# Two small reads ahead of and behind the load of c at the start of a DiT block

## The chip, the cores and the metric

The kernel runs on one core of one Trainium2 chip. The metric is the device time of one execution in microseconds; where several executions are given, it is their median. The profile is of one further execution, recorded by the hardware profiler; times in it count from the first instruction (the start of the span).

The engines are named as the profile names them: PE (TensorE: matmuls and transposes; PEld is its weight load), DVE (VectorE), ACT (ScalarE), POOL (GpSimd) and SP (SyncE, which only issues DMAs here). ACT and SP each issue DMAs on a queue of their own, q10 and q1 in the profile.

## The reference

The reference is one block of a diffusion transformer with adaptive layer norm, for 2 batches of 256 tokens, width D = 1152, 2 heads of 576, and an MLP of width 4608:

```python
mod = (_silu(c) @ w_mod).reshape(B, 6, 1, D)
shift_a, scale_a, gate_a, shift_m, scale_m, gate_m = [mod[:, i] for i in range(6)]
h = _layernorm(x, axis=-1) * (1 + scale_a) + shift_a
qkv = (h @ wqkv).reshape(B, N, 3, H, Dh)
q, k, v = (qkv[:, :, 0].copy(), qkv[:, :, 1].copy(), qkv[:, :, 2].copy())
attn = _softmax(jnp.einsum('bqhd,bkhd->bhqk', q, k) * Dh ** (-0.5), axis=-1)
a = jnp.einsum('bhqk,bkhd->bqhd', attn, v).reshape(B, N, D) @ wo
x = x + gate_a * a
h2 = _layernorm(x, axis=-1) * (1 + scale_m) + shift_m
m = _gelu(h2 @ w_fc1) @ w_fc2
return x + gate_m * m
```

All inputs are bfloat16. c has only 2 rows of 1152 values, but everything after the first layer norm depends on it through mod.

## The kernel before, in words

Tokens are held in four tiles of 128 partitions: tile t holds batch t // 2, and partition p of batch b holds the tokens 2p and 2p + 1, so one partition's two tokens are 4608 contiguous bytes in memory and one tile's row is 2304 bytes. Weights are held as nine chunks of 128 rows (KD = 9).

All weights and x are loaded by SP, in the order in which the program lists them: the four tiles of x in the order 0, 1, 3, 2 (L86), then alternating pieces of w_scale_a (the columns of w_mod for scale_a, L107) and of w_k (the K columns of wqkv, rows of chunk 0, chunk 1, then pairs of chunks, L104), then w_shift_a, w_q, w_gate_a, w_v, w_o and the rest. SP does nothing else, so that this order is the order of its queue. ACT issues the load of c (c_sb, 18 rows of 256 bytes, L84) as its first instruction, then loads its table of functions (L153).

The order of work on every engine is the order in which the program calls it: a loop at the end of the kernel ties each instruction to the one before it on its engine. At the start, that order is:

- PE: two warming matmuls of zeros in float32 (L173; each is two records in the profile, so 4), the transpose of c into pc (L176), seven more warming matmuls (14 records), the transposes of the first chunks of the normalized x of batch 0 (L264), the products of w_scale_a with silu(c) for chunks 0 and 1 (L245, L247), then the K projection in steps over the chunks (L280), with further transposes and scale groups between the steps.
- ACT: the load of c, the table load, the exponential of pc for silu (L178), then the sum and the sum of squares of x tile 0 (L206, two passes with a read of the accumulator after each), the square roots by logarithm and exponential (L335, L351, L338), then the same for tile 2.
- DVE: the rest of silu (L179 to L181, which writes sT), the statistics of x tile 1 (L193, L195), a small product for tile 0 (L213), the statistics of tile 3, then the normalizations xn of tiles 1 and 0 (L233), later of 3 and 2, and the modulations.
- POOL: constants, and small steps of the means and roots.

So tiles 0 and 2 get their statistics on ACT and tiles 1 and 3 on DVE. The lines of the load and of the transpose of c:

```python
nc.scalar.dma_start(c_sb[:], c_v)                                   # L84
...
warm(2, pwarm)
nc.tensor.transpose(pc[:], c_sb[:], ident[0:B * KD, 0:B * KD])      # L176
nc.scalar.activation(sig[:], pc[:], ACT.Exp, scale=-1.0)            # L178
...
warm(7, pwarm)
act_stats(0)
```

Completion of DMAs from ACT and SP is counted on eight semaphores, which the framework hands out in turn over all of these DMAs in program order; a DMA that gets a semaphore again waits, on the engine that issues it, for the DMA that had it before, unless a wait already made covers that.

The pieces that the diff touches and what is around them:

Of the kernel before, what the change touches and what calls it, by code (L numbers as in the profile page):

```python
# [9 lines left out]
BF16 = mybir.dt.bfloat16  # L10
# [9 lines left out]
def kernel(  # L20
# [11 lines left out]
    nc = tc.nc  # L32
    B, N, D = x.shape
# [3 lines left out]
    P = 128  # L37
    T = B * N
    NT = T // P
    TPB = N // P  # L40
# [13 lines left out]
    act = ctx.enter_context(tc.tile_pool(name="act", bufs=1))  # L54
# [12 lines left out]
    x_v = x.rearrange("b (p l) d -> p b l d", l=TPB)  # L67
    out_v = out.rearrange("b (p l) d -> p b l d", l=TPB)
    c_v = c.rearrange("b (k p) -> (b k) p", p=P)
    wqkv_v = wqkv.rearrange("(k p) n -> p k n", p=P)  # L70
# [10 lines left out]

    x_sb = act.tile([P, NT, D], BF16, name="x_sb", tag="x_sb")
    c_sb = act.tile([B * KD, P], BF16, name="c_sb")
    nc.scalar.dma_start(c_sb[:], c_v)  # L84
    for t in (0, 1, 3, 2):
        nc.sync.dma_start(x_sb[:, t, :], x_v[:, t // TPB, t % TPB, :])  # L86

# [769 lines left out]
```

## Time and profile before

| | |
|---|---|
| median of 3 runs | 243.67 us (243.65 to 243.99) |
| the profiled execution | 243.19 us |
| its span, first to last instruction | 241.4 us |
| PE busy | 236.4 us, 98% of the span |
| DVE / ACT / POOL busy | 91.4 / 59.9 / 28.3 us |
| queue q1 (SP): packets, MB | 41312, 50.14 |
| queue q10 (ACT): packets, MB | 6939, 1.71 |
| TensorE clock granted | 1.000 |

The profiled execution's time holds the span and what lies around it (1.8 us). The page gives shares over the whole span; for a change in the first two microseconds the timeline of the first stretch says more, because it shows in what order the engines take up their work and what each was waiting for: in brackets after an instruction stand the idle time before it and what ended it. "ACTq" and "SPq" rows are the issuing of DMAs by ACT and SP; the length is that of the issuing, not of the transfer. A matmul's end is modelled, so that neighbouring PE rows can overlap.

The loads at the start, with issue and time from issue to landing:

| load | issued at, us | issue to landing, us |
|---|---|---|
| x tile 0, first of four on SP | 0.73 | 2.9 |
| x tiles, all four | 0.73 to 2.1 | 2.9 to 4.9 |
| c, on ACT | 0.73 | first used at 3.18 |
| w_scale_a, first piece | 2.58 | 6.4 |
| w_k, chunk 0 | 3.06 | 6.5 |

### The profile page before, as it was taken

How to read it: one execution, taken by the hardware profiler on the slowest of the kernel's cores; microseconds unless marked ns; L12 is line 12 of the kernel's file. 1: busy time of each engine (PE TensorE's matmuls, PEld its weight loads, DVE VectorE, ACT ScalarE, POOL GpSimd, SP SyncE). 2: the span in 40 equal slices, each digit the busy share in tenths (PEclk: the TensorE clock that was granted, in tenths of full speed). 3: DMA queues.
4: the chain of work that ended last, by engine and by line, in shares of the span. 5: the costliest groups of instructions: out<-in, count | busy, mean ns of one | idle time of the engine just before them, and what ended most of it. 6: DMA issues, size and time to landing. Idle time of an engine off the chain costs nothing.

```text
span 241.4 us, 3978 instructions
## 1 busy us (share of the span) xinstructions
PE 236.4 (98%) x1688; PEld 145.1 (60%) x1698; DVE 91.4 (38%) x193; ACT 59.9 (25%) x121; POOL 28.3 (12%) x47
## 2 busy tenths in 40 slices
PE   8999999999999999999999999999999999999994
PEld 5775444466667665888844444444665566666574
DVE  4842442319325678930003999950010000000001
ACT  6723322307215032770423333222000000000000
POOL 2300000001300324100000000001121111111111
PEclk9999999999999999999999999999999999999999
DMA  6999999997499993739999999999300000000000
GB/s 196 325 317 311 377 366 391 391 391 244 122 331 394 389 274 76 195 65 378 391 391 391 337 326 270 287 327 270 98 16 16 20 16 16 19 18 20 26 21 16
DMA packets 48781, 53.29 MB, mean 221 GB/s; under 512 B 9587, under 2 KB 36475, under 8 KB 48763
## 3 DMA queue, kind: packets, MB, share of 16 engines
q1 hardware_dynamic: 41312, 50.14, 62.5%
q10 hardware_dynamic: 6939, 1.71, 4.6%
q0 software_dynamic: 512, 1.19, 1.8%
q8 instruction: 13, 0.21, 0.4%
q14 instruction: 5, 0.04, 0.1%
HBM read 50.14 MB, written 1.19 MB: 213 GB/s over the span
## 4 chain that ended last, share of the span: by engine, by line
PE 94%; issue 2%; ACT 2%; POOL 1%; DVE 0%; POOLq 0%; DVEq 0%; ACTq 0%
PE pacc L802 29%; PE pacc L746 29%; PE pacc L693 7%; PE pacc L599 7%; PE pq L521 7%; PE pk L280 5%; PE pk L309 2%; PE pa L640 2%; PE ps_s L556 2%; PE pn L416 2%; ACT sink L206 1%; PE pt L264 1%; PE pm L247 1%; PE pg L498 0%; ACT rstd L335 0%
## 5 line engine op out<-in xcount | busy, mean ns | idle before, releaser
L746 PE MATMUL pacc<-hT,w_f 128*128 128x256 bf16 (+1 forms) x427 | 70.3, 325 | 0.3
L802 PE MATMUL pacc<-w_f,gT 128*128 128x384 bf16 (+2 forms) x468 | 70.5, 314 | 0.0
L802 PEld LDWEIGHTS <-gT 128*128 128x128 bf16 x468 | 44.4, 98 | 26.3
L746 PEld LDWEIGHTS <-w_f 128*128 128x128 bf16 x432 | 42.2, 98 | 27.6
L808 DVE TENSOR_TENSOR tmp<-pacc,gate 128x384 f32<-128x384 f32 (+2 forms) x13 | 6.8, 526 | 65.6 <-PE pacc L802 57.0
L778 ACT ACTIVATE gT<-pacc 128x512 bf16<-128x512 f32 x24 | 14.3, 597 | 32.7 <-PE pacc L746 32.7
L469 DVE SCALAR_TENSOR_TENSOR part<-w_gate_m,s,part 128x1152 f32<-128x1152 bf16 x16 | 21.4, 1412 | 0.0
L810 POOL TENSOR_TENSOR o_sb<-tmp,x 128x384 bf16<-128x384 f32 (+1 forms) x12 | 11.7, 972 | 53.9 <-DVE tmp L808 53.9
L693 PE MATMUL pacc<-w_o,big 128*128 128x384 bf16 x108 | 17.9, 326 | 0.0
L521 PE MATMUL pq<-hT,w_q 128*128 128x512 bf16 x79 | 17.7, 379 | 0.1
L599 PE MATMUL pacc<-w_v,hT 128*128 128x384 bf16 x108 | 17.7, 326 | 0.0
L599 PEld LDWEIGHTS <-hT 128*128 128x128 bf16 x108 | 10.5, 98 | 7.1 <-issue 0.2
L693 PEld LDWEIGHTS <-big 128*128 128x128 bf16 x108 | 10.4, 98 | 7.2 <-issue 0.4
L521 PEld LDWEIGHTS <-w_q 128*128 128x128 bf16 x81 | 7.8, 98 | 9.4
L280 PE MATMUL pk<-big,w_k 128*128 128x256 bf16 (+1 forms) x70 | 13.1, 324 | 0.1
L699 POOL TENSOR_TENSOR x<-tmp,x_sb 128x384 f32<-128x384 f32 x8 | 7.3, 912 | 27.0 <-DMA w_scale_m<-in_w_mod_dram 15.0
L467 DVE TENSOR_SCALAR part<-w_gate_m,s 128x1152 f32<-128x1152 bf16 x2 | 1.6, 818 | 21.9 <-DMA w_gate_m<-in_w_mod_dram 21.9
L491 POOL DMA_DIRECT2D gates_dram<-nat_v x2 | 1.1, 534 | 67.7 <-DVE nat_v L489 67.7
L280 PEld LDWEIGHTS <-w_k 128*128 128x128 bf16 x72 | 6.7, 97 | 3.7 <-issue 0.3
L767 ACT ACTIVATE gT<-pacc 128x512 bf16<-128x512 f32 x12 | 6.5, 598 | 9.1 <-PE pacc L746 9.1
L173 PE MATMUL pwarm<-zeros 128*128 128x256 f32 x18 | 7.4, 587 | 1.2 <-DVE eps_t L93 1.2
L512 POOL DMA_DIRECT2D gates_dram<-nat x4 | 2.4, 604 | 49.6 <-DVE nat L509 48.5
(102 smaller groups left out, 165.0 us busy)
## 6 DMA issues: line engine op xcount, KB each, us to landing
w_f<-in_w_fc_dram SPq DMA_DIRECT2D x12, 864.0 KB, 14.1
w_f<-in_w_fc_dram SPq DMA_DIRECT2D x3, 1728.0 KB, 7.9
w_f<-in_w_fc_dram SPq DMA_DIRECT2D x2, 2592.0 KB, 17.4
w_gate_a<-in_w_mod_dram SPq DMA_DIRECT2D x3, 864.0 KB, 12.1
w_v<-in_wqkv_dram SPq DMA_DIRECT2D x3, 864.0 KB, 13.8
w_o<-in_wo_dram SPq DMA_DIRECT2D x3, 864.0 KB, 14.0
w_shift_m<-in_w_mod_dram SPq DMA_DIRECT2D x3, 864.0 KB, 8.6
w_scale_m<-in_w_mod_dram SPq DMA_DIRECT2D x3, 864.0 KB, 13.3
```

What stands on the lines that cost most here:

```text
L173: nc.tensor.matmul(dst[:, 0:T // 2], zeros32[:, 0:P], zeros32, start=True, stop=True)
L280: nc.tensor.matmul(pk[m][:, c0:c1], w_k[:, k, m * P:(m + 1) * P], hT0[:, k, c0:c1], start=(k == 0 and c0 == 0), stop=(k == KD - 1), skip_g ...
L469: nc.vector.scalar_tensor_tensor(part[:, b, :], wg[:, k, :], s32[:, k, b:b + 1], part[:, b, :], op0=ALU.mult, op1=ALU.add,)
L521: nc.tensor.matmul(pq[m][:], w_q[:, k, m * P:(m + 1) * P], hT[:, k, :], start=(k == 0), stop=(k == KD - 1), skip_group_check=True,)
L599: nc.tensor.matmul(pacc[:], hT[:, k, t * P:(t + 1) * P], w_v[:, k, pnl * PW:(pnl + 1) * PW], start=(k == 0), stop=(k == KD - 1),)
L693: nc.tensor.matmul(pacc[:], aT[:, k, t * P:(t + 1) * P], w_o[:, k, c0:c1], start=(k == 0), stop=(k == KD - 1),)
L699: (nc.gpsimd if pool_add else nc.vector).tensor_tensor(x1[:, t, c0:c1], tmp[:], x_sb[:, t, c0:c1], op=ALU.add)
L746: nc.tensor.matmul(dst, w_f1[m // KD][:, k, ml * P:(ml + 1) * P], hT[:, k, c0:c1], start=start, stop=(k == KD - 1), **kw,)
L778: nc.scalar.activation(gT[:, m, :], pacc[:], ACT.Gelu_apprx_tanh)
L802: nc.tensor.matmul(pacc[:], gT[:, kk, t * P:(t + 1) * P], w_f2[j][:, r, c0 - n * PW:c0 - n * PW + cw], start=(kk == 0), stop=(kk == KF - 1),)
L808: nc.vector.tensor_tensor(tmp[:], pacc[:], gate_m[:, b, c0:c0 + cw], op=ALU.mult)
L810: (nc.vector if last else nc.gpsimd).tensor_tensor(o_sb[:], tmp[:], x1[:, t, c0:c0 + cw], op=ALU.add)
```

## The change

Two tiles are added, touch_x and touch_k, each of 128 partitions by 2 pieces of 32 bfloat16 values (64 bytes), and two loads on ACT's DMA queue that fill them. Nothing reads either tile.

- touch_x is issued ahead of c. It views batch 1's x with a partition's two tokens as 72 pieces of 64 bytes and reads piece 0 and piece 71: the first and the last 64 bytes of each partition's 4608.
- touch_k is issued behind c. It reads 64 bytes, the first 32 of the K columns, from each of the rows 0 to 255 of wqkv (chunks 0 and 1).

Each is 256 pieces of 64 bytes, 16 KB in all. ACT issues three DMAs instead of one before its table load; the order of instructions on PE, DVE, POOL and SP is otherwise as it was. With two more DMAs, the semaphores of all later ones move on by two places: the first load of w_k now waits for touch_x, the second for x tile 0, and the third piece of w_scale_a for touch_k.

```diff
     x_sb = act.tile([P, NT, D], BF16, name="x_sb", tag="x_sb")
     c_sb = act.tile([B * KD, P], BF16, name="c_sb")
+    touch_x = act.tile([P, 2, 32], BF16, name="touch_x")
+    x_edges = x_v[:, 1, :, :].rearrange("p l d -> p (l d)").rearrange("p (s w) -> p s w", w=32)
+    nc.scalar.dma_start(touch_x[:], x_edges[:, 0:TPB * D // 32:TPB * D // 32 - 1, :])
     nc.scalar.dma_start(c_sb[:], c_v)
+    touch_k = act.tile([P, 2, 32], BF16, name="touch_k")
+    nc.scalar.dma_start(touch_k[:], wqkv_v[:, 0:2, D:D + 32])
     for t in (0, 1, 3, 2):
         nc.sync.dma_start(x_sb[:, t, :], x_v[:, t // TPB, t % TPB, :])
```

## The prediction

> **What bounds the kernel now.** I read four views, from the whole to the place of the change. First the page, for the bound:
>
> ```profile
> span 241.4 us, 3978 instructions
> PE 236.4 (98%) x1688; PEld 145.1 (60%) x1698; DVE 91.4 (38%) x193; ACT 59.9 (25%) x121; POOL 28.3 (12%) x47
> ```
>
> TensorE is busy for 98% of the span. The chain of waits runs over PE without a break longer than 0.05 us from 11.03 us to the drain. In the list of waits no PE or weight-load row names a DMA, apart from one on c. So the time is the moment at which TensorE's real work starts, plus a block of fixed length. Loads that arrive earlier inside that block buy nothing; a later start of it is paid in full.
>
> Second, the timeline of the first 10 us, for what sets that start (start, length, engine, line):
>
> ```profile
> 0.73 0.62 ACTq L84 DMA_DIRECT2D c_sb<-in_c_dram  x1
> 0.73 1.81 SPq L86 DMA_DIRECT2D x_sb<-in_x_dram  x4
> ...
> 3.18 0.10 PEld L176 LDWEIGHTS <-c_sb 18*128 18x128 bf16 x1 [0.65 <-DMA c_sb<-in_c_dram]
> ...
> 3.30 5.34 PE L173 MATMUL pwarm<-zeros 128*128 128x256 f32 x14
> 3.41 0.19 ACT L178 ACTIVATE sig<-pc 128x18 f32<-128x18 bf16 x1 [0.74 <-PE pc L176]
> 3.63 0.18 DVE L179 TENSOR_SCALAR sig<-sig 128x18 f32<-128x18 f32 x1 [2.50 <-ACT sig L178]
> 3.63 1.25 ACT L206 ACTIVATE sink<-x_sb 128x1152 f32<-128x1152 bf16 x1
> ...
> 4.38 1.48 DVE L193 BATCH_NORM_STATS2 stats<-x_sb 128x6 f32<-128x384 bf16 x3
> ...
> 6.22 1.48 DVE L193 BATCH_NORM_STATS2 stats<-x_sb 128x6 f32<-128x384 bf16 x3
> ...
> 7.89 0.67 DVE L233 TENSOR_SCALAR xn<-x_sb,mv,rstd 128x512 bf16<-128x512 bf16 x2
> ...
> 8.61 0.40 PE L264 MATMUL pt<-ident,xn 128*128 128x128 bf16 x4
> ```
>
> The transpose of c at 3.18 is the start gun for three engines. Behind it PE has 14 clock-warming records, 3.30 to 8.64. ACT has the exponential at 3.41 and, in program order behind it, the statistics of x tile 0. DVE has the three small operations on sig from 3.63, then statistics, aggregates and the two normalizations with no idle time over 0.1 us, until 8.56. All three meet at 8.61, where the first transposes of x start. None has slack worth more than 0.1 us, so c late by D means TensorE late by D.
>
> Third, the DMA view of three short windows, for how c's 18 packets (queue q10) get through beside x (q1): first 1.7 to 1.9 us, then 1.9 to 2.4, then 2.4 to 2.6. The first two numbers are packets and MB.
>
> ```profile
> q1 hardware_dynamic: 7, 0.02, 55.8%
> q10 hardware_dynamic: 20, 0.00, 8.8%
> ...
> q1 hardware_dynamic: 42, 0.10, 71.0%
> q10 hardware_dynamic: 1, 0.00, 0.2%
> ...
> q1 hardware_dynamic: 29, 0.07, 91.0%
> q10 hardware_dynamic: 6, 0.00, 2.2%
> ```
>
> Of 27 records (18 of data, 9 of completion) 20 are through before x has properly arrived. The last 6 come only after 2.4, half a microsecond and 42 x packets later. A short transfer is thus quick on an empty queue and slow once x packets stand beside it.
>
> Fourth, sums over stretches, for what the touching could repair (the last two columns are DMA share and GB/s):
>
> ```profile
> 2.25:3.50 1.25, 1.25 (x5) 0.58 (x4) 0.00 (x0) 0.51 (x2) 0.21 (x3) 1.00 0.98 355
> 3.50:5.25 1.75, 1.75 (x5) 1.39 (x6) 1.48 (x5) 1.68 (x4) 0.00 (x0) 1.00 1.00 248
> 5.25:7.00 1.75, 1.75 (x6) 1.39 (x5) 1.63 (x6) 1.60 (x4) 0.48 (x2) 1.00 0.99 311
> ```
>
> While batch 1's x starts, the DMA engines are as busy as before (1.00) but move 248 GB/s in place of 355: packets stall. That costs (355-248)/355 x 1.75 = 0.5 us of DMA time.
>
> **What the skill says.** The Trainium skill, "DMA: Bandwidth & Descriptors", section "Issuing engines are not separate DMA queues": what the scalar and sync engines start runs on the same 16 DMA engines and interleaves. The third view agrees. Its section "Queues, rings and completion order" says that each engine goes round-robin between the rows at packet granularity and keeps ring order inside a row; how many descriptors go in one turn it leaves wide, and the windows here don't settle it. Its section "Why a DMA increments its semaphore by 16 and not by 1" says the number of engines is the largest up to 16 that divides the outer dimension: 9 for c's 18 rows (the 9 completion records agree), 16 for the touch loads' 128 partitions, so 16 packets on each engine. "TensorE: Matmul & The Clock Gate", Part 1, says the array starts at half clock and goes to full after a busy, free-running window of about 3.4 us. The trace agrees in kind: the 18 records of L173 start about 0.43 us apart at first and 0.21 us apart from about 7.4 us on.
>
> **The change, part by part.**
>
> *touch_x, issue.* ACT now issues a 256-packet load before c. No such load is in the trace; the nearest rows are SP's x loads (1.81 us for 4, 0.45 each with its gap) and c's own 0.62. I take 0.5 us (bounds 0.4 to 0.7): c's packets reach the rings at about 2.2 instead of 1.72.
>
> *touch_x, in front of c in the ring.* At 2.2 us x is on every engine. Lower bound: the touch packets go through in a lump before x arrives, nothing is added, and even the later issue is partly covered by the wait that c's last packets have anyway (2.4 to 2.6): D = 0.3. Likely value: turns of one packet each. An x packet takes 0.10 us (2304 B at 355 GB/s over 16 engines, 22 B/ns), a q10 record some 0.01 (8.8% of 0.2 us x 16 engines over 20 records is 0.014). Sixteen touch packets with an x packet behind each: 16 x 0.11 = 1.8 us from 1.72, so 3.5; c's two packets 0.2 more, 3.7, against about 2.55 now: 1.15. The stall that batch 1 shows in the fourth view is now met by the touch packets, with c waiting behind them: of the 0.5 us I put half on c, 0.25. D = 1.4. Upper bound: each turn gives x several packets (42 x packets in the gap over 16 engines are 2.6 per engine): 18 x 0.27 = 4.9 us from 1.72, D = 4.0.
>
> *What D does.* The gun moves from 3.18 to 4.6. PE's four earlier warm records end at 3.25, which covers 0.07 us, so little that I drop it. DVE ends at 8.56 + 1.4 = 9.96 and PE's warm block at 3.30 + 1.4 + 5.34 = 10.04: together again. PE now idles 1.4 us in its warm-up, so the full clock may come later. If all 14 records ran at the slow spacing the block would take 14 x 0.427 = 5.98, 0.64 more, and nothing covers that. Bounds 0 and 0.64; half, 0.3, is my value.
>
> *touch_k and the table load.* The third issue (0.5 us) pushes the 1.28 us ACT table load from 1.39 to about 2.4 and its end to 3.7. That is before the exponential at 4.8 and hidden by the wait for c; if c came at 3.2 after all, it would cost 0.5. Its 256 packets stand behind c and delay x tiles 3 and 2 by 16 x 0.014 = 0.2 us per engine. The users of those tiles have moved by 1.4, so nothing.
>
> *Completion semaphores.* In the built program each load reuses the semaphore of the load eight before it and waits for it. With two more loads, the first w_k load (issued at 3.06) now waits for touch_x (about 4.2), the second for x tile 0, and the third w_scale_a for touch_k (about 6; issued at 7.71 now). Behind the waiting w_k on SP stand all later weight loads. But x and the first w_scale_a, 1.7 MB, are already queued, 5 us at 330 GB/s, so the DMA engines don't run dry; and the first users, w_scale_a at 9.04 and w_k at 9.62 on PE, have moved by 1.7. Cost 0; with the cover gone, up to 1.
>
> *Gain.* x of batch 1, w_scale_a and w_k may arrive up to 0.5 us sooner. Their users wait for none of them by more than 0.1 us, and they now start later. Gain 0, at most 0.3: the 0.24 us that PE idles between 8.6 and 30 us (21.39 less 21.15 busy) and DVE's 0.08.
>
> Sum: 1.4 + 0.3 + 0 - 0 = +1.7 us. The profiled execution took 243.19 us (241.4 of span and 1.8 around it), so 244.9 of that kind; it lies 0.5 below the median of the runs, to which I add the difference: 243.67 + 1.7 = **245.4 us**.
>
> **Rivals.**
>
> *Only the issue slot counts.* The touch packets leave before x arrives; D is 0.3 to 0.8: 243.9 to 244.5. For it: c's first 20 records passed within 0.2 us, and a touch packet is smaller still. Against it: c then comes when x is there, and needs the long turns of its last packets.
>
> *Long turns.* Touch packets get one turn for several of x's: +2.2 to +4.3, 246 to 248. For it: the half microsecond in which one q10 record passed against 42 of q1. Against it: some of that is stalls of x's first packets, which happen once.
>
> *Faster.* The touches take the cold stalls early, in the idle time of the rings, and c's last packets, now at 2.4 to 2.6 behind a stalled x packet, are no later than now. Then x, w_scale_a and w_k come early and PE gets its 0.3 us: 243.4; by more than 0.49 us only if undisturbed runs, which are 0.5 slower than the profiled one, lose that time to the same stalls. It decides only where D is under 0.2. Against it: c is issued 0.5 later by program order.
>
> *It does nothing.* If batch 1's stall is not one of first contact, the touch loads are mere traffic; c is delayed nonetheless, so this is the forecast less 0.25: 245.1.
>
> **How the numbers follow.** Forecast (+0.8 to +2.2) 0.55; issue slot 0.27, of which about half is under 0.49 us; long turns 0.13; faster 0.05. Two tenths of a per cent, 0.49 us, is about what a measurement of this kernel can tell from no change. So faster 0.05, within 0.15, slower 0.80. The range, 244.0 to 247.0, leaves out the faster cases and the smallest delays below and the worst of the long turns above.
>
> **What would show it.** c's transpose at 4.6 instead of 3.18, with three ACT issues before the table load; the 14 warm records, the exponential and L179 starting with it; the first x transposes at about 10.3; the same length from there to the end; more than 248 GB/s where batch 1's x starts. Wrong would be a c that lands by 3.4, or a DVE or PE that waits for x tile 1 (a bound hidden behind c), or a TensorE that makes up the delay later, which would mean that it waited on loads after all.

## The result, and the profile after

The changed kernel takes 245.03 us (244.75 to 245.31), the kernel before, measured beside it, 243.50 us (243.18 to 243.99): a ratio of 1.0062, with a 95% interval of 1.0048 to 1.0076. It is slower by 1.5 us. Measured a second time beside other kernels it was slower by 1.1 us (1.0046, 1.0033 to 1.0060). The profiled execution took 244.75 us, with a span of 243.0.

The page of the changed kernel, its first lines:

```profile
span 243.0 us, 3990 instructions
PE 236.7 (97%) x1698; PEld 144.9 (60%) x1698; DVE 91.3 (38%) x193; ACT 59.8 (25%) x121; POOL 28.3 (12%) x47
```

TensorE's busy time is nearly what it was (236.4 before). The span has grown by idle time, and the timeline of the first 10 us shows where (start, length, engine, line; line numbers are 5 higher than before):

```profile
0.73 0.48 ACTq L86 DMA_DIRECT2D touch_x<-in_x_dram  x1
...
1.24 0.64 ACTq L87 DMA_DIRECT2D c_sb<-in_c_dram  x1
...
1.92 0.40 ACTq L89 DMA_DIRECT2D touch_k<-in_wqkv_dram  x1
...
2.35 1.28 ACT L158 ACT_TABLE_LOAD   x1 [2.35 <-issue]
...
3.81 1.14 SPq L109 DMA_DIRECT2D w_k<-in_wqkv_dram  x2
4.45 0.10 PEld L181 LDWEIGHTS <-c_sb 18*128 18x128 bf16 x1 [1.92 <-DMA c_sb<-in_c_dram]
...
4.58 5.04 PE L178 MATMUL pwarm<-zeros 128*128 128x256 f32 x14
4.68 0.19 ACT L183 ACTIVATE sig<-pc 128x18 f32<-128x18 bf16 x1 [1.05 <-PE pc L181]
...
9.63 0.40 PE L269 MATMUL pt<-ident,xn 128*128 128x128 bf16 x4
```

The transpose of c has moved from 3.18 to 4.45 us, 1.27 later; the first transposes of x from 8.61 to 9.63, 1.02 later. The next view is the chain of work that ended last, in order of time (start, length, what). It shows what gates TensorE in this execution: ACT's statistics and roots of tile 2, its normalization, its transposes.

```profile
8.42 1.25 ACT sink L211 x2
...
9.69 1.36 ACT sink L211 x2
...
11.13 0.30 ACT rstd L340
...
11.75 0.42 DVE xn L238
...
12.22 0.28 PE pt L269 x2
```

Those transposes were at 11.03 before: 1.19 later. From there the shift is constant. The first matmul of the last projection starts at 169.15 instead of 167.96 (1.19), and the last DVE operation at 239.88 instead of 238.68 (1.20). Another 0.4 us of the span lies behind that operation, where SP waits for the last store to land. The list of SP's waits, first of the kernel before, then of the change (us, times, longest):

```profile
SPq L852 <- DMA out_dram<-o_sb: 0.6, 1, 0.6
...
SPq L857 <- DMA out_dram<-o_sb: 1.0, 1, 1.0
```

This is no accident of one execution. In all thirteen profiles of this case the store itself takes the same time, 1.43 to 1.45 us from issue to landing, but the time from the start of the last DVE operation to the end of the span depends on how many loads a kernel has: 2.72 to 2.73 us with no touch load, 2.66 to 2.68 with one, and 3.09 in all four profiles with both. The traces show why. At the end SP checks the completion semaphores one after the other, some 0.06 us apart, the eight of the loads and stores always from the lowest number to the highest. Each added load moves the last store on by one semaphore. Before, the store has the last but one of the eight in that order, and with one load more the last; with two more the numbering begins again, and it has the first. SP then stands at this early check until the store has landed, and makes the others afterwards instead of meanwhile: the checks are through 0.14 us after the landing before, 0.08 with one more load and 0.51 with two. So 0.37 us of the change's cost has nothing to do with c or with the touched data.

How c got through shows in the DMA view, for five stretches of the changed kernel: 1.7 to 1.9, 1.9 to 2.4, 2.4 to 2.9, 2.9 to 3.4, and 3.4 to 3.9 us (packets, MB, share of 16 engines; q10 is ACT's queue, q1 is SP's):

```profile
q1 hardware_dynamic: 14, 0.03, 97.5%
...
q1 hardware_dynamic: 33, 0.08, 78.4%
...
q1 hardware_dynamic: 78, 0.16, 85.2%
q10 hardware_dynamic: 83, 0.01, 11.3%
...
q1 hardware_dynamic: 81, 0.17, 87.8%
q10 hardware_dynamic: 202, 0.01, 28.2%
...
q1 hardware_dynamic: 88, 0.18, 100.8%
q10 hardware_dynamic: 14, 0.00, 2.5%
```

No record of q10 is seen before 2.4 us; in the kernel before, 20 of c's 27 were through by 1.9. Then the touch packets come in a lump: 202 records of q10 in half a microsecond against 81 of q1, at 11 ns each (28.2% of 0.5 us x 16 engines over 202). The last of c follows after 3.4.

Last, the stretches in which batch 1's x arrives (last two columns: DMA share and GB/s):

```profile
2.25:3.50 1.25, 1.00 (x3) 0.28 (x1) 0.00 (x0) 1.15 (x1) 0.22 (x3) 1.00 0.99 329
3.50:5.25 1.75, 0.80 (x3) 0.69 (x4) 0.32 (x2) 0.70 (x3) 0.00 (x0) 1.00 0.95 300
5.25:7.00 1.75, 1.75 (x6) 1.39 (x5) 1.64 (x5) 1.72 (x3) 0.00 (x0) 1.00 0.97 287
```

The middle one has 300 GB/s where it had 248, which looks like the repair that the touching suggests. The experiments say otherwise.

### The profile page after: what moved, and what is told of

It is laid out like the page before. It is cut to its first block, busy times and chain, and to the rows that moved or that the text cites. A ratio compares the mean times of both kernels' runs of the same rounds, so it can differ in the third digit from the quotient of the medians.

```text
span 243.0 us, 3990 instructions
## 1 busy us (share of the span) xinstructions
PE 236.7 (97%) x1698; PEld 144.9 (60%) x1698; DVE 91.3 (38%) x193; ACT 59.8 (25%) x121; POOL 28.3 (12%) x47
## 3 DMA queue, kind: packets, MB, share of 16 engines
q0 software_dynamic: 512, 1.19, 1.5%
HBM read 50.17 MB, written 1.19 MB: 211 GB/s over the span
## 4 chain that ended last, share of the span: by engine, by line
PE 94%; issue 2%; ACT 2%; POOL 1%; DVE 0%; POOLq 0%; DVEq 0%; ACTq 0%
PE pacc L807 29%; PE pacc L751 29%; PE pacc L698 7%; PE pacc L604 7%; PE pq L526 7%; PE pk L285 5%; PE pk L314 2%; PE pa L645 2%; PE ps_s L561 2%; PE pn L421 2%; ACT sink L211 1%; PE pt L269 1%; PE pm L252 1%; PE pg L503 0%; ACT rstd L340 0%
```

## The experiments

In each, "time" is the ratio to the kernel before, measured beside it, turned into microseconds with that kernel's median (243.59 to 243.72). Beside the first four experiments, 52 executions of the kernel before span 243.11 to 244.43, so the execution profiled before (243.19) is one of its fastest; that matters below. Where c's transpose and other moments are given, they are those of the one profiled execution.

**c first.** The same two loads, behind c.

```diff
+    nc.scalar.dma_start(c_sb[:], c_v)
     nc.scalar.dma_start(touch_x[:], x_edges[...])
-    nc.scalar.dma_start(c_sb[:], c_v)
     nc.scalar.dma_start(touch_k[:], wqkv_v[:, 0:2, D:D + 32])
```

> The same two touch loads, but c is issued ahead of both. Theory (c is the start gun, and the touch loads cost only by standing ahead of it): c's transpose is back at 3.2 us, and the time is that of before, within 0.3 us; a gain of up to 0.3 us is possible because batch 1's x comes sooner. Rival (the touch packets cost by their traffic and by the waits on their semaphores, wherever they stand): half or more of the 1.5 us stays, 244.3 us or more.

Measured: ratio 1.0026 (1.0015 to 1.0036), +0.6 us. c's transpose is at 3.18, as the theory wants, yet 0.6 us stays. The list of waits of this kernel, first of ACT and then of PE, shows a path that the prediction held to be free (who waited for what: us, times, longest):

```profile
ACT sink L211 <- DMA x_sb<-in_x_dram: 0.5, 1, 0.5
...
PE pm L252 <- DMA w_scale_a<-in_w_mod_dram: 0.8, 1, 0.8
```

So most of the cost goes when c is first. Of the 0.6 us that stay, 0.37 is the later end that every kernel with both touch loads has; the rest, some 0.3, fits the loads that come late, and is within what the theory allowed. In this profile the chain that ended last runs through the first piece of w_scale_a, which lands 7.28 us after its issue at 2.57, and not through c. One thing more is late: behind three issues the table load ends at 3.61, so that the exponential starts at 3.62 instead of 3.41, and ACT's statistics at 3.72 instead of 3.63.

**touch_x alone, ahead of c.** The change without its last two lines.

> touch_x ahead of c, no touch_k. Theory: touch_k, behind c, costs nothing, so this is as slow as the full change, +1.5 us within 0.3. Rival: touch_k and its issuing share the cost; then +1.0 us or less.

Measured: 1.0023 (1.0015 to 1.0031), +0.6 us, with c's transpose at 4.27. The interval doesn't touch that of both loads, so touch_k is not free in company. But this kernel has one more load and not two, and so the early end: 0.43 us of the difference from the change is that.

**A tiny touch_x.** One packet for each DMA engine, ahead of c, and no touch_k. Against the change:

```diff
-    touch_x = act.tile([P, 2, 32], BF16, name="touch_x")
+    touch_x = act.tile([16, 1, 32], BF16, name="touch_x")
...
-    nc.scalar.dma_start(touch_x[:], x_edges[:, 0:TPB * D // 32:TPB * D // 32 - 1, :])
+    nc.scalar.dma_start(touch_x[:], x_edges[0:16, 0:1, :])
```

> touch_x cut to 16 packets of 64 bytes (one for each DMA engine), ahead of c, no touch_k. Theory A, that the queues take turns by whole loads (an engine's whole share of one load goes through before the other queue gets its turn, as the touch packets that follow each other without a gap in the changed kernel suggest): the number of touch packets matters little, c is still behind a turn of x, c's transpose at 4.0 to 4.5 us and +0.8 to +1.3 us. Theory B, that they take turns packet by packet (the step of the prediction): 15 turns of 0.11 us fewer, what is left is the issue slot, c's transpose at about 3.5 and +0.2 to +0.5 us.

Measured: 1.0003 (0.9994 to 1.0011), no difference, with c's transpose at 3.67. By the delay of c this is theory B; but 202 records of q10 against 81 of q1 in half a microsecond, above, are not turns packet by packet, and the run with four times the packets, below, is far from B. What this run does show is that in it 0.5 us of delay of c costs next to nothing in time.

**The table load first.** No touch load; the lines of the table load are moved ahead of c's load.

> No touch load at all; ACT loads its table of functions ahead of issuing c, so that c is issued 1.3 us later. Theory (a late c is the whole cause): c's transpose between 4.3 and 5.2 us, and the time rises by as much as the transpose is late, less some 0.1 us: +1.0 to +1.9. Rival (the touch packets matter in themselves, and a late c is partly covered): less than half of the transpose's delay shows in the time.

Measured: 1.0000 (0.9990 to 1.0009). The experiment didn't make c late: the timeline shows the two side by side,

```profile
0.73 1.28 ACT L85 ACT_TABLE_LOAD   x1 [0.73 <-PEq L841]
...
0.76 0.61 ACTq L89 DMA_DIRECT2D c_sb<-in_c_dram  x1
```

so here the table load didn't hold back the issuing of the DMA behind it. The run tells the theories apart no further, but gives a second look at what is in effect the kernel before, at 243.90 us. There c's transpose is at 3.23 and TensorE waits for a load after all:

```profile
PE pm L247 <- DMA w_scale_a<-in_w_mod_dram: 0.4, 1, 0.4
```

In this execution the chain that ended last doesn't pass through c at all: it is SP's issuing of the weight loads up to a piece of w_scale_a that is issued at 11.05 and lands 8.80 us later.

**The change again.**

> The changed kernel unaltered, beside the others of this call. touch_x alone gave +0.5 us where 1.5 was measured for both touch loads. If touch_k matters, this stays 0.7 us or more above before; if the first measurement of 1.5 was high by the spread of the runs of before (243.1 to 244.4), it falls to +0.5 to +0.9.

Measured: 1.0046 (1.0033 to 1.0060), +1.1 us; c's transpose at 4.54, 1.36 late. Both of its measurements together put the cost at 1.1 to 1.5 us. In this second profile ACT's chain for tile 2 isn't the last to end. The chain that ended last begins, in order of time, with a load, SP's issuing and another load (three of its pieces: start, length, what):

```profile
0.73 2.79 DMA touch_x<-in_x_dram
...
3.54 0.46 SPq L109
...
11.98 8.79 DMA w_scale_a<-in_w_mod_dram
```

SP waits for touch_x's semaphore before it issues the first piece of w_k (3.54 instead of 3.06), everything behind it on SP comes later (for this, and because the next issuing for w_k takes 3.33 us instead of 2.25), and at the end of it TensorE waits 0.2 us for a piece of w_scale_a.

**touch_k alone, behind c.**

> touch_k alone, behind c. Theory of the prediction: its traffic is covered, 0 within 0.2 us. Rival, after the run with c first showed TensorE waiting 0.8 us for w_scale_a: the stream of loads is a second path as long as c's, and 256 packets between x tile 0 and tile 2 lengthen it: +0.2 to +0.6 us, with TensorE waiting for w_scale_a or ACT for x tile 2.

Measured: 0.9990 (0.9978 to 1.0003), no difference that can be told. Its profile has TensorE waiting 0.5 us for w_scale_a, as a kernel without any touch load has it too.

**A very late c.** No touch load; c's load is listed further down, with those of x behind it, and waits for a POOL operation and, through its semaphore, for x tile 0.

```diff
-    nc.scalar.dma_start(c_sb[:], c_v)
...
+    held = nc.gpsimd.tensor_tensor(early[:], eps_t[:], neg_half[:, 0:1], op=ALU.pow)
+    c_load = nc.scalar.dma_start(c_sb[:], c_v)
+    tc.add_manual_dep(c_load.ins, held.ins.name, WAIT_FOR, reason="late c")
...
-    nc.gpsimd.tensor_tensor(early[:], eps_t[:], neg_half[:, 0:1], op=ALU.pow)
```

> No touch load; c's load is held until a POOL operation and x tile 0 are done, so that it is issued at about 3.6 us instead of 0.7 and its transpose comes at 5.5 to 6. Theory (c starts everything, the loads' lateness in a run of before covers at most 0.5 us of it): the time rises by the transpose's delay less 0 to 0.5, so +1.8 to +2.6. Rival (a late c is mostly covered and the touch packets themselves cost): +1.2 or less.

Measured: 1.0223 (1.0209 to 1.0237), +5.4 us, and c's transpose at 9.04, 5.86 late. The size is off because c, issued at 3.64, waited far longer than I assumed. The DMA view of this kernel for 3.6 to 7.4 and for 7.4 to 8.5 us:

```profile
q1 hardware_dynamic: 1295, 1.11, 96.9%
...
q1 hardware_dynamic: 380, 0.37, 108.7%
q10 hardware_dynamic: 27, 0.00, 2.8%
```

Not one of c's packets ran while 1295 packets of x and weights went past, 81 for each of 16 engines. The relation holds nonetheless: 5.4 us of time for 5.86 of delay, again some 0.4 less.

**Touching batch 0.** touch_x reads batch 0's pieces.

```diff
-    x_edges = x_v[:, 1, :, :].rearrange(...)
+    x_edges = x_v[:, 0, :, :].rearrange(...)
```

> touch_x reads the same pieces of batch 0 in place of batch 1, all else as in the change. If batch 1's stall is one of first contact, it is back: 230 to 270 GB/s between 3.5 and 5.25 us and not 300. c stands behind the same number of packets, so its transpose comes at 4.0 to 4.6; the time is that of the full change within 0.4 us, for a late c covers the stall. If first contact were the cost to c, its transpose would come by 0.4 us or more sooner than in the change.

Measured: 1.0041 (1.0028 to 1.0054), +1.0 us; c's transpose at 4.35. The stretch of batch 1's arrival, which nothing touched here:

```profile
3.50:5.25 1.75, 0.90 (x3) 0.79 (x4) 0.42 (x2) 0.84 (x3) 0.00 (x0) 1.00 1.00 315
```

315 GB/s, more than with batch 1 touched (300 and, again, 274). Without any touch load the same stretch has 248 (before), 336 (table first) and 280 (the slot alone, below). The slow stretch varies between executions and doesn't follow what is touched; these runs give no sign that first contact is its cause, and with one profile of each kernel they don't rule it out.

**Four times the packets.** touch_x with 8 pieces, no touch_k: `x_edges[:, 0:TPB * D // 32:9, :]`.

> touch_x with 8 pieces of 64 bytes for each partition in place of 2 (64 packets on each DMA engine), ahead of c, no touch_k. Turns by whole loads: 48 more packets at 7 ns each add 0.34 us, c's transpose at 4.5 to 5.0 us, the time +1.0 to +1.6. Turns of at most some 16 descriptors: three more turns of x at 0.75 us, c's transpose at 6 to 7 and +2.3 to +3.5. Turns packet by packet: 48 x 0.11, c's transpose at 9 or later.

Measured: 1.0065 (1.0052 to 1.0078), +1.6 us; c's transpose at 5.19. Packet by packet is out. The DMA view for 2.4 to 3.4, 3.4 to 3.9 and 3.9 to 4.6 us:

```profile
q1 hardware_dynamic: 118, 0.24, 63.2%
q10 hardware_dynamic: 520, 0.03, 35.5%
...
q1 hardware_dynamic: 78, 0.18, 91.6%
q10 hardware_dynamic: 98, 0.01, 13.4%
...
q1 hardware_dynamic: 103, 0.20, 74.5%
q10 hardware_dynamic: 449, 0.03, 44.8%
```

The packets come in two lumps of about half, with x between. If every engine's share of 64 went that way, a turn holds some thirty of them, or the second half was written to the rings later (this load and c took 1.5 us to issue); the runs don't tell which, and the view sums over the 16 engines. c's transpose lies between the two expectations left, 0.2 above the nearer.

**The slot alone.** No touch load; c is held until DVE's memset of the epsilon tile ends, and is issued at 1.18 (1.24 in the change).

```diff
-    nc.scalar.dma_start(c_sb[:], c_v)
...
-    nc.vector.memset(eps_t[:], LN_EPS)
+    held = nc.vector.memset(eps_t[:], LN_EPS)
...
+    c_load = nc.scalar.dma_start(c_sb[:], c_v)
+    tc.add_manual_dep(c_load.ins, held.ins.name, WAIT_FOR, reason="late c")
```

> No touch load; c's load is held until DVE's memset of the epsilon tile ends at 1.1 us, so that c is issued at about 1.2 us, as in the change. If the issue slot alone accounts for what 16 packets of touch_x did, c's transpose comes at 3.5 to 3.8 us and the time is that of before within 0.3 us; then the touch packets themselves account for the rest of the change's delay (4.45 less 3.65). If the slot accounts for the whole, c's transpose comes at 4.2 or later and +0.6 or more.

Measured: 1.0014 (1.0005 to 1.0022), +0.3 us; c's transpose at 3.61. Of the change's delay of 1.27 the issue slot is thus about 0.43, and 0.84 is left for the touch loads' packets; touch_x alone, at 1.09, leaves 0.66.

**c first, then touch_x alone.**

> c first, then touch_x, no touch_k. With both behind c the time was +0.6, with touch_k alone behind c -0.2. If touch_x's turn between x tiles 0 and 2 lengthens the path of the loads, TensorE waits for w_scale_a or ACT for x tile 2 and the time is +0.3 to +0.7 with c's transpose at 3.2. If it takes both touch loads, it is within 0.2 us of before.

Measured: 1.0003 (0.9993 to 1.0013), no difference, c's transpose at 3.18. Behind c each touch load alone is free, and both together cost 0.6, of which 0.37 is the later end. For the rest, some 0.3: with both, the second w_scale_a is issued at 5.31 (4.64 with the table load first) and the third at 8.58 (7.90). That fits the wait for touch_x's semaphore, which the second has only there; whether the semaphore or the traffic makes it late was not separated.

## Why the prediction was right, and which steps of it were not

In order of c's transpose. The time is in microseconds above before; the last column is without what the end of the kernel adds or saves by the number of loads (+0.37 with both touch loads, -0.06 with one). It takes the end of the one profiled execution for that of all.

| kernel | c's transpose, us | later than 3.18 | time | without the end |
|---|---|---|---|---|
| touch_k alone behind c | 3.18 | 0 | -0.2 | -0.2 |
| touch_x alone behind c | 3.18 | 0 | +0.1 | +0.1 |
| both behind c | 3.18 | 0 | +0.6 | +0.3 |
| table load first | 3.23 | 0.05 | 0.0 | 0.0 |
| slot alone | 3.61 | 0.43 | +0.3 | +0.3 |
| tiny touch_x | 3.67 | 0.49 | +0.1 | +0.1 |
| touch_x alone | 4.27 | 1.09 | +0.6 | +0.6 |
| batch 0 touched | 4.35 | 1.17 | +1.0 | +0.6 |
| the change, and again | 4.45, 4.54 | 1.27, 1.36 | +1.5, +1.1 | +1.2, +0.8 |
| four times the packets | 5.19 | 2.01 | +1.6 | +1.6 |
| very late c | 9.04 | 5.86 | +5.4 | +5.4 |

*A late c is a late TensorE: right.* From 1 us of delay upward the time without the end follows the delay, in kernels with and without touch loads, some 0.4 to 0.6 us below it (one profile for each delay); only the first measurement of the change is nearer, 0.1 below. A little slack was there at once, against the prediction's "none": x tile 0 lands at about 3.6, so that before ACT's statistics start 0.22 us after the exponential, and in the change 0.08. So ACT's chain moved by 1.13 at its start, and the transposes of tile 2 by 1.19, not by 1.27.

*The size of the delay, 1.4: nearly right (1.27 and 1.36), for partly wrong reasons.* The issue slot was taken as 0.5; touch_x occupied ACT for 0.48, and the slot alone delays c by 0.43. The step that failed is the next one: sixteen turns of one packet each, 0.11 us a turn, from 1.72 us on. (The prediction had called the size of a turn open, and took one packet for its sum.) The touch packets start only after 2.4 us and then go through at 202 records to 81 of q1. So c's delay behind them is a late start and then a quick passage; that the late start is a wait for x's turn is likely, but not shown. Why touch_x's packets come 0.7 us or more later than c's did before, at the same time of issue, stays open. The 0.25 us for the stall that the touch packets would meet has little support: c is only 0.1 to 0.2 us earlier when batch 0 is touched, one execution against two, and no run ties the stall to batch 1.

*Half of the warm-up loss, 0.3: not seen in the change.* The 14 warm records took 5.34 us before and 5.04 and 5.40 in the change. In the run with touch_x alone they took 5.91, so that the first transposes came at 10.14 and not 9.63. But tile 2's came at 12.26 and not 12.22. ACT's second pass over tile 2 starts 0.17 us earlier there than in the change (9.52 and 9.69), so its chain would have allowed some 0.2 earlier than 12.26. ACT's chain is thus the cover that the step lacked: it hides most of the loss; some 0.2 comes through, and the chain that ended last in that profile runs over the warm records.

*The loads are not free: the step on the gain failed.* The list of waits of before showed no wait of TensorE for a load, but it was of one of that kernel's fastest executions. In two others with c at 3.2 (table load first, touch_k alone) TensorE waits 0.4 and 0.5 us for w_scale_a, in a third (touch_x alone behind c) 0.2, and in all three the chain that ended last runs through a load and not through c. So there are two paths of nearly the same length, c's and that of the loads. The 0.48 us between the profiled execution and the median, added as a constant, is about the size of that waiting. A late c hides it: the first profile of the change has none of these waits, the second 0.2 us, and those of the other kernels with c after 4 us none. That is the likely reason why time stays below delay by 0.4 us or more. That the waiting makes up the whole of the 0.48 is inferred, not shown.

*touch_k and the completion semaphores at nothing: right alone, wrong in company.* Alone behind c, touch_k costs nothing; with touch_x it adds 0.5 us or more (+0.6 against +1.1 and +1.5). The prediction followed the semaphores to the first weight loads only. It did not follow them to the last store, where the second added load brings the numbering round to the first semaphore: 0.37 us above before, 0.43 above touch_x alone. About 0.2 more is c's transpose (4.27 against 4.45 and 4.54). These two make up the difference within its spread. At the start, the second profile of the change has the cost "with the cover gone" that the prediction named: there the wait for touch_x's semaphore lies on the chain that ended last, and TensorE waits 0.2 us at its end. In the first profile it doesn't.

The forecast of +1.7 thus stands against 1.5 and 1.1. That it is so near is partly luck: the 0.3 of warm-up didn't come and some 0.4 of cover was missed, and the 0.37 at the end, which the prediction didn't have, made up for half of that. In the profiled pair the work ends 1.20 later, not 1.7. The rival of the issue slot alone gave 243.9 to 244.5; the kernel that has only the slot took 243.92, but the change is not that kernel. Long turns in the rival's sense (c past 6 us) occurred only where c was issued at 3.6, into a queue full of weights.

## What to carry to other kernels

A load that every engine's first work depends on should be issued first, on an empty queue. Here half a microsecond later cost it 0.43 us by itself, 1.1 to 1.4 with 256 small packets ahead of it in its own queue, and 5.86 when it was issued at 3.64 us behind the bulk loads. A profile without waits for loads can come from one fast execution of a kernel whose loads arrive just in time; compare its own time with the spread of the runs before calling the loads covered. A dip of the DMA rate in one execution is not yet a place to repair. And an added DMA can cost time far from where it stands: compare the last instructions of both kernels too, from the last operation to the end of the span.

## What the runs showed of the hardware

- ACT's table load (1.28 us) ran beside the issuing of a DMA behind it in ACT's program: c's load was issued at 0.76 us while the table load ran from 0.73 to 2.01.
- A load of 18 packets of 256 bytes, issued at 3.64 us behind queued bulk loads, had no packet through before 7.4 us, while 1295 packets of the other queue passed.
- Packets of 64 bytes took 11 ns each of a DMA engine's time and didn't go in turns of one with the other queue's: 202 records of q10, most of them such packets, went beside 81 of q1 in half a microsecond.
- The same 14 matmul records took between 3.93 us (c first, touch_x alone) and 5.91 us (touch_x alone, ahead of c). Their starts were 0.43 us apart at first and 0.22 later, and the step from one to the other came after the third record in the first kernel and only at the last in the second.
- The last store landed 1.43 to 1.45 us after its issue in all thirteen profiles, and SP's checks of the semaphores, some 0.06 us each, were through 0.08 to 0.51 us after that, by the place of the store's semaphore in their order.
